# Dense batch 0 in units of 128 tokens, batches 1 to 3 of a block-sparse attention by lists of key blocks

## The chip, the core and the metric

The kernel runs on one core of one Trainium2 chip. The core has TensorE (PE, matmuls, with its weight loads shown apart as PEld), VectorE (DVE), ScalarE (ACT), GpSimd (POOL) and SyncE (SP, which here only issues DMAs). Each engine works through its own instructions in program order and waits on semaphores for the others. The metric is the device time of one execution in microseconds (us); less is better. Several executions of a kernel are timed, and the median is given with the lowest and the highest.

## What is computed

A BigBird-like attention over 4 batches, 8 heads, 768 tokens and head size 64, followed by a SwiGLU feed-forward network (FFN) on 3072 tokens of width 512.

```python
block, n_blocks, window = 32, 24, 1
scores = q @ k^T / sqrt(64)
mask = |blk_i - blk_j| <= 1
mask |= blk_i in (0, 23) or blk_j in (0, 23)
for qb in range(24):
    for kb in sampled_blocks[qb]:          # 3 per query block, drawn at random, an input
        mask[rows of qb, columns of kb] = True
attn = softmax(where(mask, scores, -1e9)) @ v
x = attn, heads side by side: [3072, 512]
xn = x / sqrt(mean(x*x) + 1e-6) * rms_g
out = (silu(xn @ w_gate) * (xn @ w_val)) @ w_out      # 512 -> 1536 -> 512
```

A query block of 1 to 22 thus sees at most 8 key blocks of 24: its own, two neighbours, blocks 0 and 23, and three sampled ones (which can coincide with the others). Blocks 0 and 23 see all keys. Inputs are fp32; matmuls are in bf16.

## The kernel before

**Tiling.** Tokens are laid out so that partition p of 128 holds the six tokens 6p to 6p+5 (`"b h (p c) d -> b p h (c d)"`, L66), and a tile c is one token of each partition. Work goes by units (L51): batch 0 has units of 1, 1, 1 and 3 tiles (128, 128, 128 and 384 tokens), batches 1 to 3 have two units of 384 tokens. A pair is two heads; there are four pairs.

**Attention is dense.** All 768 keys are scored for all queries, and the mask is put in by the matmul itself: to the 64 rows of K are appended 24 rows that say which block a key is in, and to those of Q 24 rows with 0 or -32768, so that the contraction has 88 rows (`KQ`). `qk` (L268) makes the scores in two PSUM banks, for 384 tokens one matmul of 384 columns per head and key tile; `exp` (L281) takes them through ACT into the tile `pt`, two heads x 384 columns at a time; `av` (L301) multiplies with V, which has a 65th column of ones that sums the probabilities; `xo` (L315) divides by that sum on DVE.

**Feeding it.** For batch 0, K and Q are cast into `aug` and transposed on TensorE (`tpx` L252, `evx` L261). For batches 1 to 3 they are loaded a pair at a time from SP's queue (`load` L76, 12 pairs x 3 loads), cast on DVE (`fill` L234, `pad_v` L238) and transposed by a DMA issued on SP (`turn` L244, 12 of them).

**FFN.** For each unit: `sq` (L326, DVE) and `rsq` (L339, POOL) make the norm, `xq` (L346, DVE) scales, the result is transposed on TensorE (`tr`, `cp`) for the first four units and by DMA (`xt` L373) for the rest. Then come steps f, each of 384 columns: `proj` (L380) with the gate weights into bank 4, `th` (L393, tanh on ACT), `uu` (L399, DVE, which frees bank 4), `proj` with the value weights into bank 5, `hp` (L407, DVE). `yy` (L418) and `yo` (L431) make and store the output. Near the end, when all scores are made, the banks of the scores serve the FFN too (L689).

**Order.** All of it is put in order by a planner in the kernel's Python (L458 to L768): each operation has a cost per engine, dependencies, a priority and buffers or banks that it takes and gives back; a list scheduler with assumed latencies (`LAT`, L455) picks the next operation, and the instructions are issued in that order. SP's queue has an order of its own (`seq`): loads of batch 0, then checks that weight chunks have landed (`gate_sync`, L218), then the loads of later batches, with output stores, transposes and these loads all behind one another. POOL issues the ten weight DMAs and casts a few tiles at the start; after that it only has `rsq`.

Of the kernel before, what the change touches and what calls it, by code (L numbers as in the profile page):

```python
# [17 lines left out]
def kernel(  # L18
# [11 lines left out]
):  # L30
    nc = tc.nc
    SIMOUT = None
# [12 lines left out]
    NSLOT, NAUG, NRAW, NOPEN = 5, 2, 3, 2  # L45
# [5 lines left out]
    UNITS = [(0, 0, 1), (0, 1, 1), (0, 2, 1), (0, 3, 3)]  # L51
    UNITS += [(b, c, 3) for b in range(1, B) for c in (0, 3)]
    NU = len(UNITS)
    HG = [(b, c // 3) for b, c, n in UNITS]
# [3 lines left out]
    raw = ctx.enter_context(tc.tile_pool(name="raw", bufs=NRAW))  # L58
    work = ctx.enter_context(tc.tile_pool(name="work", bufs=2))
    psum = ctx.enter_context(tc.tile_pool(name="psum", bufs=1, space=bass.MemoryType.PSUM))  # L60
    PS = psum.tile([P, 8, 512], FP32, name="PS")

# [7 lines left out]
    raws = {}  # L70
    aug = [const.tile([P, 2, 2, NC, P], BF16, name=f"aug{i}") for i in range(NAUG)]
    XA = const.tile([P, NSLOT, 2, 2, S], BF16, name="XA")
    X = [XA[:, i] for i in range(NSLOT)]
    vaug = [const.tile([P, H * NC, D + 2], BF16, name=f"vaug{i}") for i in range(2)]

    def load(g, i):  # L76
        b, pr = divmod(g, NP)
        if i == 0:
            raws[g] = raw.tile([P, 3, 2, NC * D], FP32, name="qkv", tag="qkv")
        nc.sync.dma_start(out=raws[g][:, i], in_=(kv, qv, vv)[i][b, :, 2 * pr:2 * pr + 2, :])  # L80
# [9 lines left out]
    A = [raw.tile([P, 3, 2, NC * D], FP32, name="qkv", tag="qkv") for g in range(3)]  # L90
# [23 lines left out]
    zt = const.tile([P, 512], BF16, name="zt")  # L114
# [11 lines left out]
    def idle(n, bk=7):  # L126
# [23 lines left out]
        base=-(NB - 1), pattern=[[0, 32]], channel_multiplier=1)  # L150
    kt_ = bank16(4)[:, 0:S].rearrange("p (c t) -> p c t", t=P)
# [8 lines left out]
    for t in vaug:  # L160
        nc.vector.memset(t[:, :, D:D + 1], 1.0)
# [72 lines left out]
    def fill(g, i, eng):  # L234
        copy(eng, aug[g % NAUG][:, i, :, :, 0:D],
             raws[g][:, i].rearrange("p h (c d) -> p h c d", d=D))

    def pad_v(g, eng):  # L238
        b, pr = divmod(g, NP)
        src = raws.pop(g) if b else A[g]  # L240
        copy(eng, vaug[b % 2][:, 2 * pr * NC:2 * (pr + 1) * NC, 0:D],
             src[:, 2].rearrange("p h (c d) -> p (h c) d", d=D))

    def turn(g):  # L244
        nc.sync.dma_start_transpose(
            out=X[g % NSLOT].rearrange("p i e (c t) -> p (i e c) t", t=P),
            in_=aug[g % NAUG].rearrange("p i e c r -> p (i e c r)"))

    def zero_pad(i):
        nc.vector.memset(aug[i][:, :, :, :, KQ:P], 0.0)  # L250
# [13 lines left out]

    pts, xos, xns, hps, mss, xqs, tiles = {}, {}, {}, {}, {}, {}, {}
    KT, FG = {1: 3, 2: 2, 3: 1}, {1: 3, 2: 2, 3: 1}

    def qk(u, pr, g, bk):  # L268
        b, c0, nt = UNITS[u]
        x, kt, w = X[(b * NP + pr) % NSLOT], KT[nt], nt * P  # L270
# [10 lines left out]
    def exp(u, pr, g):  # L281
        b, c0, nt = UNITS[u]
        kt, w = KT[nt], nt * P
        if (u, pr) not in pts:
            if nt == 1:
# [4 lines left out]
                else:  # L290
                    t_ = work.tile([P, 2, NC, 2, w], BF16, name="pt", tag="pt", bufs=NPT)
                pts[u, pr // 2 * 2], pts[u, pr // 2 * 2 + 1] = t_[:, 0], t_[:, 1]
            else:
                pts[u, pr] = work.tile([P, NC, 2, w], BF16, name="pt", tag="pt", bufs=NPT)
# [6 lines left out]
    def av(u, pr, bk):  # L301
        b, c0, nt = UNITS[u]
        pt, va = pts.pop((u, pr)), vaug[b % 2]
# [11 lines left out]
    def xo(u, pr):  # L315
        nt = UNITS[u][2]
        if u not in xos:
            xos[u] = work.tile([P, nt, H, D], FP32, name="xo", tag="xo")
# [7 lines left out]
    def sq(u, t):  # L326
# [5 lines left out]
        if nt == 1:  # L332
            z = (slice(0, 3 * DM // 4), slice(3 * DM // 4, DM))[t]
# [30 lines left out]
    def cp(u, eng):  # L364
# [3 lines left out]
        if eng == "ACT":  # L368
            nc.scalar.copy(out=o, in_=i)
        else:  # L370
            nc.vector.tensor_copy(out=o, in_=i)
# [428 lines left out]
```

## Time and profile before

| | |
|---|---|
| median of 3 runs | 309.45 us (308.69 to 309.54) |
| span of the profiled execution | 307.2 us |
| TensorE: granted clock | 0.999 |
| TensorE matmul busy, 30 to 60 us | 29.8 us |
| TensorE matmul busy, 130 to 210 us | 79.4 us |
| DMA engines busy in slices 2 to 16 of 40 (8 to 123 us) | 90% or more each |
| last matmul of the scores | 221.7 us |
| FFN alone after that | to 303.3 us |

The span is from the first to the last instruction of one execution; the timed median is a little longer than it. Busy times of an engine leave out instructions that only issue DMAs, except on POOL, where the issue is work of the engine. The group rows give, after the shapes and the count, the summed busy time, the mean duration of one in ns, and, after the second bar, the idle time of the engine just before them and what ended it.

### The profile page before, as it was taken

The numbers are of one execution on the slowest core, as the hardware profiler recorded it, in microseconds if no ns is written. First come the engines' busy times: TensorE is split into PE (matmuls) and PEld (weight loads), VectorE is DVE, ScalarE is ACT, GpSimd is POOL, SyncE is SP. The second block draws the span as 40 slices with busy tenths as digits, with TensorE's granted clock in tenths as the row PEclk, the third lists the DMA queues.
The fourth block names the chain that finished last, engine by engine and source line by source line (L and its number), as shares of the span: only waits on it lengthen the run. The fifth ranks groups of instructions, "written<-read, shape, count | busy, mean of one in ns | idle before, by whom it ended". The sixth has DMA issues, their size and how long they took to land.

```text
span 307.2 us, 7350 instructions
## 1 busy us (share of the span) xinstructions
PE 299.6 (98%) x3033; PEld 200.2 (65%) x3062; DVE 192.3 (63%) x435; ACT 203.7 (66%) x319; POOL 24.4 (8%) x43
## 2 busy tenths in 40 slices
PE   8999999999999999999999999999999999999994
PEld 7998888766666566666666666666666546556543
DVE  6687766857779678756754753674389607727500
ACT  5999875678977878787877787878833143233221
POOL 3566000100001001001000100010000000000000
PEclk9999999999999999999999999999999999999999
DMA  7999999999999999940894030003010050010022
GB/s 207 370 231 172 215 268 228 228 333 247 262 285 271 227 205 222 242 155 3 173 157 101 0 87 2 34 3 85 2 36 1 20 158 12 0 70 0 0 105 104
DMA packets 70661, 42.42 MB, mean 138 GB/s; under 512 B 48356, under 2 KB 67556, under 8 KB 70628
## 3 DMA queue, kind: packets, MB, share of 16 engines
q1 hardware_dynamic: 64528, 37.17, 49.2%
q0 software_dynamic: 5792, 4.72, 10.0%
q8 instruction: 24, 0.39, 0.6%
q10 hardware_dynamic: 308, 0.07, 0.1%
q14 instruction: 9, 0.07, 0.1%
HBM read 28.57 MB, written 6.29 MB: 114 GB/s over the span
## 4 chain that ended last, share of the span: by engine, by line
PE 96%; ACT 2%; issue 1%; DVE 0%; ACTq 0%
PE PS L388 40%; PE PS L276 20%; PE PS L427 20%; PE PS L310 12%; PE PS L258 2%; ACT pt L296 1%; PE PS L128 1%; PE PS L361 0%; ACT th L397 0%; PE PS L153 0%; ACT yo L437 0%; PE PS L183 0%; DVE zt L115 0%; ACTq L437 0%
## 5 line engine op out<-in xcount | busy, mean ns | idle before, releaser
L296 ACT ACTIVATE pt<-PS 128x768 bf16<-128x768 f32 x188 | 142.8, 812 | 32.2 <-PE PS L276 31.5
L403 DVE SCALAR_TENSOR_TENSOR uu<-th,PS 128x384 bf16<-128x384 bf16 x96 | 53.0, 554 | 58.7 <-ACT th L397 55.7
L276 PE MATMUL PS<-XA 88*128 88x384 bf16 (+1 forms) x480 | 81.1, 293 | 0.7 <-ACT pt L296 0.6
L388 PE MATMUL PS<-xn,wv 128*128 128x384 bf16 (+1 forms) x480 | 75.5, 293 | 0.0
L388 PE MATMUL PS<-xn,wg 128*128 128x384 bf16 (+1 forms) x480 | 75.1, 294 | 0.0
L397 ACT ACTIVATE th<-PS 128x384 bf16<-128x384 f32 x96 | 47.2, 493 | 34.8 <-PE PS L388 32.1
L427 PE MATMUL PS<-wo,hp 128*128 128x512 bf16 (+1 forms) x271 | 65.4, 370 | 1.5
L414 DVE TENSOR_TENSOR hp<-uu,PS 128x384 bf16<-128x384 bf16 x96 | 51.4, 551 | 14.2 <-PE PS L388 14.0
L388 PEld LDWEIGHTS <-wv 128*128 128x128 bf16 x480 | 41.6, 97 | 23.3
L388 PEld LDWEIGHTS <-wg 128*128 128x128 bf16 x480 | 41.4, 98 | 22.5
L276 PEld LDWEIGHTS <-XA 88*128 88x128 bf16 x480 | 39.2, 97 | 21.4 <-issue 1.8
L427 PEld LDWEIGHTS <-hp 128*128 128x128 bf16 x300 | 29.1, 98 | 27.0
L310 PEld LDWEIGHTS <-pt 128*128 128x128 bf16 x1128 | 40.5, 97 | 5.8
L310 PE MATMUL PS<-vaug,pt 128*128 128x65 bf16 x1128 | 42.1, 193 | 0.0
L437 ACT ACTIVATE yo<-PS 128x512 f32<-128x512 f32 (+1 forms) x22 | 12.7, 578 | 27.9 <-PE PS L427 27.2
L343 POOL TENSOR_TENSOR rs<-ms,nhalf 128x3 f32<-128x3 f32 (+1 forms) x10 | 7.9, 785 | 203.8 <-DVE ms L335 203.8
L322 DVE TENSOR_TENSOR xo<-PS,rz 128x384 f32<-128x384 f32 (+1 forms) x40 | 19.1, 478 | 1.4
L350 DVE SCALAR_TENSOR_TENSOR xq<-xo,rs,gB 128x512 bf16<-128x512 f32 x24 | 17.3, 747 | 2.3 <-POOL rs L343 2.3
L335 DVE CUSTOM_DVE_ANT_0 sc<-xo 128x512 bf16<-128x512 f32 (+1 forms) x24 | 16.1, 669 | 0.2
L321 DVE RECIPROCAL rz<-PS 128x6 f32<-128x6 f32 (+1 forms) x40 | 7.4, 186 | 12.8 <-PE PS L310 12.6
L112 DVE CAST aug<-qkv 128x768 bf16<-128x768 f32 (+1 forms) x28 | 14.5, 538 | 0.1
L112 DVE COPY XA<-PS 88x768 bf16<-88x768 bf16 (+2 forms) x17 | 8.4, 516 | 2.3 <-PE PS L258 2.2
(60 smaller groups left out, 74.5 us busy)
## 6 DMA issues: line engine op xcount, KB each, us to landing
out_dram<-yo SPq DMA_DIRECT2D x23, 256.0 KB, 2.4
qkv<-in_v_dram SPq DMA_DIRECT2D x15, 384.0 KB, 6.1
qkv<-in_k_dram SPq DMA_DIRECT2D x14, 384.0 KB, 5.6
qkv<-in_q_dram SPq DMA_DIRECT2D x12, 384.0 KB, 5.7
wg<-in_moe_w_gate_dram POOLq DMA_DIRECT2D x4, 384.0 KB, 7.3
wv<-in_moe_w_val_dram POOLq DMA_DIRECT2D x4, 384.0 KB, 8.4
wo<-in_moe_w_out_dram POOLq DMA_DIRECT2D x2, 768.0 KB, 19.0
q<-in_q_dram SPq DMA_DIRECT2D x1, 768.0 KB
```

The costliest lines, as they stand in the source:

```text
L112: nc.vector.tensor_copy(out=out, in_=in_)
L276: nc.tensor.matmul(out=s_[:, e, j * w:(j + 1) * w], lhsT=x[0:KQ, 0, e, jt * P:(jt + 1) * P], rhs=x[0:KQ, 1, e, c0 * P:c0 * P + w], start=T ...
L296: nc.scalar.activation(out=pts[u, pr][:, g * kt:(g + 1) * kt].rearrange("p j e w -> p e j w"), in_=s_[:, :, 0:kt * w].rearrange("p e (j w) ...
L310: nc.tensor.matmul(out=o_[:, t, e, :], lhsT=pt[:, jt, e, t * P:(t + 1) * P], rhs=va[:, (2 * pr + e) * NC + jt, 0:D + 1], start=(jt == 0), ...
L322: nc.vector.tensor_tensor(out=xos[u][:, :, 2 * pr:2 * pr + 2, :], in0=o_[:, :, :, 0:D], in1=rz.unsqueeze(3).to_broadcast([P, nt, 2, D]), o ...
L335: nc.vector.tensor_tensor_reduce(out=sc[:, z], in0=x, in1=x, scale=1.0 / DM, scalar=mss[u][:, 0:1] if nt == 1 and t else 1e-6, op0=ALU.mul ...
L350: nc.vector.scalar_tensor_tensor(out=xqs[u][:, t, :], in0=xos[u][:, t].rearrange("p h d -> p (h d)"), scalar=mss[u][:, t:t + 1], in1=gB, o ...
L388: nc.tensor.matmul(out=p_[:, j, :].rearrange("p (t w) -> p t w", w=P), lhsT=w_[:, c, f_ * P:(f_ + 1) * P], rhs=xns[u][:, :, c, :], start=( ...
L397: nc.scalar.activation(out=t_, in_=tiles["gp", u, f], func=AF.Tanh, scale=0.5)
L403: nc.vector.scalar_tensor_tensor(out=t_, in0=tiles.pop(("th", u, f)), scalar=1.0, in1=tiles.pop(("gp", u, f)), op0=ALU.add, op1=ALU.mult)
L414: nc.vector.tensor_tensor(out=hps[u][:, f * fg:(f + 1) * fg, :], in0=tiles.pop(("uu", u, f)), in1=tiles.pop(("vp", u, f)), op=ALU.mult)
L427: nc.tensor.matmul(out=tiles["yp", u, t, h], lhsT=hps[u][:, f, t * P:(t + 1) * P], rhs=wo[:, f, x], start=(f == 0), stop=(f == NF - 1))
```

## The change

Batch 0 keeps the dense code (renamed `dk`, `dexp`, `dav`, `dxo`) but has six units of 128 tokens in place of 128, 128, 128 and 384. Its three large probability tiles come from one fixed tile.

Batches 1 to 3 are sparse. Their tokens lie in natural order, 128 rows to a group; a group n is four query blocks: 4n+1 to 4n+4 for n from 0 to 4, and blocks 0, 23, 21, 22 for group 5 (`AT`). A batch has two units of three groups, (5, 0, 1) and (2, 3, 4).

- **Keys.** K of a batch is loaded whole (512-byte pieces), cast and transposed by one DMA (`turn_k`); two heads are stacked in the 128 rows. For each group a tile `kg` is filled by copies with six slots of 128 keys: slots 0 to 3 hold, for each query block, three sampled blocks and one neighbour; slots 4 and 5 hold, for each two query blocks, those two blocks and blocks 0 and 23. The sampled copies read K at an offset from a register, on POOL (samples 0 and 1) or ACT (sample 2).
- **Queries.** Q (256-byte pieces) is transposed on TensorE for batch 1 and by DMA for batches 2 and 3, and copied into a tile `QBD` with the two heads side by side and zeros in the other head's rows.
- **Scores and probabilities.** `qk` makes matmuls of 64 columns (slots 0 to 3) and 128 columns (slots 4 and 5). `exp` writes them into tiles that were set to zero once, so that queries a slot does not concern have probability zero. Group 5 scores all keys for blocks 0 and 23 (`qka`, `expa`).
- **Values.** V is cast, stored to DRAM as rows of 520 bf16 (8 heads of 64 and a one), and fetched back by list: a slot of 128 rows by one indirect DMA on POOL (`gather_v`), slots 4 and 5 by SP (`pair_v`). A sampled block that coincides with another of the list is pointed at a block of zero rows, which takes the place of the mask.
- **Table.** The row numbers (`idx`) are computed once on DVE and POOL, and 66 block offsets are loaded into registers of POOL (44) and ACT (22) near planned time 48 us.
- **Around it.** The square of `sq` may run on ACT; `rsq` has two instructions; `NXN` goes from 3 to 2; output of group 5 is stored in three pieces; six units (those of batch 0) transpose on TensorE.

```diff
-    UNITS = [(0, 0, 1), (0, 1, 1), (0, 2, 1), (0, 3, 3)]
-    UNITS += [(b, c, 3) for b in range(1, B) for c in (0, 3)]
+    DENSE = [(c, 1) for c in range(NC)]
+    UNITS = [(0, c, n) for c, n in DENSE]
+    for b in range(1, B):
+        UNITS += [(b, (5, 0, 1), 3), (b, (2, 3, 4), 3)]
...
+    def turn_k(b):
+        KTs[b] = KTB[held["KT", b][1]]
+        nc.sync.dma_start_transpose(
+            out=KTs[b].rearrange("p a (n x) -> p (a n) x", x=P), in_=KROW.rearrange("p a c t x -> p (a c t x)"))
...
+    def kg_sampled(b, n, xs, eng):
+        kg = new_kg(b, n).rearrange("p x a s j c -> p x a c s j")
+        kt = KTs[b].rearrange("p a (c y) -> p a c y", c=2)
+        for x, r in xs:
+            kb = koff[(blocks(n)[x] - 1) * NR + r]
+            copy(eng, kg[:, x, :, :, r, :], kt[:, :, :, bass.ds(kb, 16)])
...
+    def gather_v(b, n, x):
+        c_ = blocks(n)[x] - 1
+        nc.gpsimd.indirect_dma_start(
+            out=new_vg(b, n)[:, x, :], out_offset=None, in_=vrows[b][:, :],
+            in_offset=bass.IndirectOffsetOnAxis(ap=idx[:, c_:c_ + 1], axis=0))
...
+    def qk(b, n, pp, bk):
+        s_ = PS[:, bk[0]:bk[0] + 2].rearrange("p k (h x) -> p (k h) x", h=2)
+        tiles["s", b, n, pp] = s_
+        kg = kgs[b, n].rearrange("p x a s j c -> p x a (s j c)")
+        qb = tiles["qb", b, n]
+        for pl in range(2):
+            pr = 2 * pp + pl
+            o_ = s_[:, 2 * pl:2 * pl + 2]
+            for i in range(4):
+                qmm(o_[:, :, i * 32:(i + 1) * 32], kg[:, i, pr], qb, i, 1, pr)
+            for g in range(2):
+                lo = P + g * 64
+                qmm(o_[:, :, lo:lo + 64], kg[:, 4 + g, pr], qb, 2 * g, 2, pr)
...
+    def av(b, n, pp, bk):
+        p_, vg = pts.pop((b, n, pp)), vgs[b, n]
...
+        for a in range(4):
+            h = 4 * pp + a
+            if n == AT:
+                vs = [vaug[:, m % 3, m // 3, h, :] for m in range(NC)]
+                vs += [vg[:, x, h * (D + 1):(h + 1) * (D + 1)] for x in (2, 3, 5)]
+            else:
+                vs = [vg[:, x, h * (D + 1):(h + 1) * (D + 1)] for x in range(6)]
+            for x, v_ in enumerate(vs):
+                nc.tensor.matmul(
+                    out=o_[:, a, :], lhsT=p_[:, a, x * P:(x + 1) * P], rhs=v_,
+                    start=(x == 0), stop=(x == len(vs) - 1))
...
-        nc.gpsimd.tensor_tensor(out=r, in0=x, in1=nhalf[:, 0:nt], op=ALU.pow)
+        nc.gpsimd.tensor_scalar(out=r, in0=x, scalar1=1e-6, scalar2=None, op0=ALU.add)
+        nc.gpsimd.tensor_tensor(out=r, in0=r, in1=nhalf[:, 0:nt], op=ALU.pow)
...
+    done0 = [("av", u, pr) for u in (ND - 2, ND - 1) for pr in range(NP)]
...
+    for i in range(NPT + 1 + NQB):
+        op(("zr", i), {"DVE": 1.3, "POOL": 1.9} if i <= NPT else {"DVE": 0.7, "POOL": 1.1},
+           done0 if i <= NPT else [("dk", ND - 1, 2, ng3 - 1)], (3.5, i), lambda e, p, i=i: zero(i, e))
...
+            op(("pvi",) + T, {"SP": 2.0}, [("st", b)], (1.1, order),
+               lambda e, p, a=T: pair_v(*a), [("vg", T)])
...
+            for x in xs:
+                op(("gv",) + T + (x,), {"POOL": 1.05}, [("st", b), ("ix", 7)], (1.1, order, x),
+                   lambda e, p, a=T + (x,): gather_v(*a), [("vg", T)])
+                op(("gd",) + T + (x,), {"DMA": 0.4}, [("gv",) + T + (x,)], (-1, order, x), None)
```

## The prediction

> **What bounds the kernel now.** I read the page's busy shares first, then the chain that ended last, then the groups with shapes kept apart, then the chain in order of time for the price of single matmuls.
>
> ```profile
> span 307.2 us, 7350 instructions
> PE 299.6 (98%) x3033; PEld 200.2 (65%) x3062; DVE 192.3 (63%) x435; ACT 203.7 (66%) x319; POOL 24.4 (8%) x43
> ...
> PE PS L388 40%; PE PS L276 20%; PE PS L427 20%; PE PS L310 12%; PE PS L258 2%; ACT pt L296 1%; PE PS L128 1%; PE PS L361 0%; ACT th L397 0%; PE PS L153 0%; ACT yo L437 0%; PE PS L183 0%; DVE zt L115 0%; ACTq L437 0%
> ```
>
> TensorE works 98% of the span and is 96% of the chain. 7.6 us are left to idling. So a microsecond of matmul removed is a microsecond won, as long as the next engine in line keeps TensorE fed.
>
> ```profile
> 31.70 1.15 PE PS L310 x36
> 32.85 0.65 PE PS L276 x4
> ...
> 27.61 0.67 PE PS L388 x12
> ...
> 241.07 10.31 PE PS L427 x47
> ```
>
> In the chain by time (start, duration, what) I take prices of single matmuls: 65 columns with a new weight each 1.15/36 = 0.032 us; 384 columns 0.65/4 = 0.1625; 128 columns 0.67/12 = 0.056; 512 columns 10.31/47 = 0.219. The means in the groups (325 ns for 384 columns) are latencies of overlapping matmuls and would double the sum.
>
> ```profile
> L296 ACT ACTIVATE pt<-PS 128x768 bf16<-128x768 f32 x188 | 142.8, 812 | 32.2 <-PE PS L276 31.5
> L403 DVE SCALAR_TENSOR_TENSOR uu<-th,PS 128x384 bf16<-128x384 bf16 x96 | 53.0, 554 | 58.7 <-ACT th L397 55.7
> L397 ACT ACTIVATE th<-PS 128x384 bf16<-128x384 f32 x96 | 47.2, 493 | 34.8 <-PE PS L388 32.1 <-ACT pt L296 0.2
> L322 DVE TENSOR_TENSOR xo<-PS,rz 128x384 f32<-128x384 f32 x28 | 15.6, 557 | 1.0
> L343 POOL TENSOR_TENSOR rs<-ms,nhalf 128x3 f32<-128x3 f32 x7 | 6.1, 878 | 199.7 <-DVE ms L335 199.7
> L211 POOL DMA_DIRECT2D wg<-in_moe_w_gate_dram x4 | 3.3, 818 | 0.0
> L110 POOL CAST aug<-qkv 128x256 bf16<-128x256 f32 x1 | 0.4, 400 | 0.4 <-DMA qkv<-in_q_dram 0.4
> ```
>
> These rows price the other engines. POOL is all but idle now (8%); the change hands it the most.
>
> **TensorE, batches 1 to 3.** Removed: 3 batches x 2 units x 4 pairs x 2 heads x 6 key tiles = 288 score matmuls of 384 columns, 288 x 0.1625 = 46.8 us. Added per batch: five ordinary groups with, per pair, 4 matmuls of 64 columns and 2 of 128, so 4 x (4 x 0.032 + 2 x 0.056) = 0.96 us each, 4.8 in all; the group with blocks 0 and 23 has per pair 7 of 128 and 2 of 64, 4 x 0.456 = 1.8. That is 6.6 a batch, 19.9 for three. **Saving 26.9.** AV grows from 288 to 5 x 48 + 72 = 312 matmuls a batch: 72 x 0.032 = +2.3. Q of batch 1 is now transposed on TensorE: 24 x 0.056 = +1.3. K of 128 rows (was 88) costs nothing: the AV rows have 128 and are the price used.
>
> **TensorE, batch 0.** Unit 3 (384 tokens) becomes three of 128: 96 projections 15.6 -> 288 x 0.056 = 16.1, and 48 scores 7.8 -> 144 x 0.056 = 8.1: +0.8. Sum: 299.6 - 26.9 + 2.3 + 1.3 + 0.8 = 277.1 us. With the 7.6 of idle as now the span is 284.7. The shown median, 309.45, is 2.25 above this execution's span; I carry that over: **286.9 if nothing else idles TensorE**. The FFN and the tail of outputs are unchanged.
>
> **What must keep pace with it.** TensorE has per sparse batch 192 x 0.1625 + 72 x 0.219 + 6.6 + 312 x 0.032 = 63.5 us (71.9 now). Against that:
> ACT. Two rows (384 columns 493 ns, 768 columns 812) give 0.174 + 0.83 ns per column, so 512 columns 0.60, 256 0.39, 128 0.28. Exps: 20 x 0.60 + 4 x (0.60 + 0.39 + 0.28 + 0.28) = 18.2 a batch (48 x 0.76 = 36.5 now). Added: third sampled key, 11 operations of two 128-column copies, 22 x 0.28 = 6.2. With tanh 24 x 0.49 and outputs 6 x 0.6: 39.8.
> DVE. uu and hp 24 x 1.105 = 26.5; xo, now 12 of 256 columns, 12 x (0.19 + 0.42) = 7.4, with 0.42 between the 128-column (291 ns) and 384-column rows; squares and scaling 6 x (0.77 + 0.75) = 9.1: 43.0.
> POOL. Sampled keys 22 operations of two copies, 44 x 0.30 = 13.2 (from 400 ns for 256 columns and 507 for 384); rsq, now two instructions, 2 x (0.88 + 0.4) = 2.6; 22 gathers. No row shows an **indirect DMA**: the least is a plain weight DMA issued on POOL (0.74), the most, far away, the issue of a transposing DMA on SP (median 4.37, where the issuer makes all its pieces). A gather is one DMA with one index per partition, nearest to the plain one; I take 1.05, 23.1 a batch: 38.9.
> Free to go to any of the three: casts of K, V, Q, fixed key copies, diagonal Q, about 7 + 7.7 + 4.9 = 19.6 us. In all 141 of 3 x 63.5 = 191 engine-us, 74%. Now ACT is at 52 of 71.9 and DVE at 48. So no engine binds by its total. They serve as cover as long as the gathers stay below 2.2 us, where 15.8 + 22 x 2.2 passes 63.5.
>
> ```profile
> 46.05 10.53 SPq L245 DMA_TRANSPOSE XA<-aug  x2
> ...
> 57.99 0.39 SPq L80 DMA_DIRECT2D qkv<-in_k_dram  x1
> ```
>
> **The SP queue** gains. A transposing DMA holds it for 3.6 to 6.2 us, and 12 of them become 5: 7 x 4.4 = 31 us less. Against that come, per batch, 10 loads (12 now), one store of V, 12 pair and end-block copies and 2 more output pieces: 13 more of 0.45, 6 us. The pair copies wait in that queue for a V buffer and for the store; queued behind them are next-batch loads and outputs, whose landing is needed a block later. At zero, as SP has gaps of 14 us and more after 130 us.
> **Register loads.** 66 block offsets, 22 on ACT and 44 on POOL, near 48 us. No row shows one; least 0.10 (POOL's smallest memset), most 0.44 (an SP issue): 2.2 to 9.7 us on ACT. I take 5, hidden since ACT is busy 5.4 of 10 from 50 to 60; without that cover it delays the exps of batch 0 by 5. The table itself, some 30 small DVE operations at 0.16, is 5 us in a stretch where DVE has 2 to 3 of 10 free.
>
> **The hand-over to batch 1** is the new wait I charge. The first sparse scores wait for the last dense AV (the zeros in the shared probability tiles, about 3 us on two engines), then 11 us of exps for three groups, 3 for AV and xo, 5 for square, power and scaling, 4 for the transpose: 26 us before unit 6 has an FFN. Cover: FFN of units 4 and 5, 2 x 8 = 16 us of TensorE, and 9 us of its own sparse attention. But with one bank for g, a step lasts 0.67 + 0.2 + 0.49 + 0.16 + 0.55 + 0.08 = 2.15 us for 1.34 of matmul (0.2, 0.16 and 0.08 are the planner's latencies), so the cover is leaky: 4 us, bounds 0 (unit 7's attention fills it) and 16 (K, V and Q of batch 1 land late). Uneven fit over 18 groups: 2 us, bounds 0 and 9 (half a DVE instruction per group; the static order was exact to 0.5% until now). 286.9 + 4 + 2 = **293**.
>
> [...] POOL's weight DMAs took 0.74 to 0.95 us beside a DVE at 7.6 of 10. [...]
>
> **Rivals.**
> 1. The chain g-th-uu in its one bank sets the pace. A step of 384 tokens is 0.65 + 0.2 + 0.49 + 0.16 + 0.55 + 0.08 = 2.13 us, 25.6 for the 12 of a unit, and TensorE has 31.8. With one and a half foreign DVE instructions of 0.55 ahead of each uu it is 2.95 x 12 = 35.4: 3.6 x 4 interleaved units = 14 us on 288: 302. For: DVE gets more, smaller work. Against: before, 3 us a step was kept with TensorE above 99%.
> 2. POOL binds (slower). Gathers can start near 50 us; three batches take 3 x (15.8 + 22 g); after the last come about 33 us of attention and FFN. 130 + 66 g passes 309.45 at g = 2.7; at the row's upper end of 4.37 it is 418, and I price the rival a little past its threshold, at 3: 328. For: 66 operations with no row behind them. Against: the plain issues at 0.8.
> 3. Batch 1 is late. Its loads now run in pieces of 256 and 512 bytes (1536 now), each group needs all of K, Q and stored V, and DMA is above 90% busy from 8 to 123 us: 16 us of idle instead of 4, 305.
> 4. Small matmuls don't shrink: at 0.1 each the 468 new scores cost 46.8, and the time is 314. The 0.032 rows speak against it; I fold it into the second.
>
> **Chances.** Forecast 0.50 (own range 284 to 300), rival 1 0.15, rival 2 with 4 0.23, rival 3 0.12. Changes under 0.3% can't be told from none. Faster: 0.49 + 0.11 + 0.01 + 0.09 = 0.70; same 0.03; slower 0.27. The range goes from 283, every bound in favour, less 4 for better packing, to 314, which takes in rivals 1 and 3 and the low edge of 2.
>
> **What would show it.** Scores of batches 1 to 3 near 20 us on TensorE, its busy time near 277; exps near 55 us there; gathers near 1.05 on POOL; an idle hole of TensorE between 60 and 85 us no longer than 6. Wrong: gathers over 2.2, TensorE below 93%, or waits for POOL key copies in the chain.

## The result: 349.43 us, and the profile after

The changed kernel takes 349.43 us (median of 4 runs, 346.68 to 352.56), the kernel before beside it 309.07: a ratio of 1.128 (95% interval 1.122 to 1.134). The ratios in this text leave out executions more than 1.5% above their kernel's fastest, the medians do not. The forecast was 293, its range 283 to 314. The profiled execution has a span of 346.2 us. First the page of the kernel after: span, busy shares, the chain that ended last, three groups.

```profile
span 346.2 us, 9294 instructions
...
PE 295.3 (85%) x3625; PEld 211.6 (61%) x3625; DVE 208.2 (60%) x525; ACT 187.0 (54%) x417; POOL 155.7 (45%) x294
...
PE 59%; DVE 9%; issue 5%; another core or an unknown queue 3%; ACT 2%; DMA 1%; ACTq 0%; DVEq 0%
...
L741 DVE SCALAR_TENSOR_TENSOR uu<-th,PS 128x384 bf16<-128x384 bf16 x96 | 52.8, 552 | 44.6 <-ACT th L735 38.3
L547 POOL DMA_INDIRECT VGC<-vrows,idx x66 | 64.5, 977 | 27.9 <-issue 13.8
...
L752 DVE TENSOR_TENSOR hp<-uu,PS 128x384 bf16<-128x384 bf16 x96 | 51.3, 551 | 29.7 <-remote 13.1
```

TensorE is busy 4.3 us less than before (295.3 against 299.6), not 22.5, and idle 50.9 us (346.2 - 295.3) where it was idle 7.6. `uu` takes 552 ns (554 before). No other engine took TensorE's place: POOL, the fullest by the change, is at 45%; its power for three tiles (`rs`) takes 940 ns (878 before). The gathers cost POOL what was said (0.977 us each). New in the page is "remote": VectorE stood 13.1 us before `hp` for an event of which the profile knows no source.

The groups of the kernel after with shapes kept apart:

```profile
L607 ACT ACTIVATE PTC<-PS 128x512 bf16<-128x512 f32 x60 | 33.2, 599 | 16.4 <-remote 6.4 <-PE PS L580 3.5 <-PE PS L726 3.5
L659 DVE TENSOR_TENSOR XO<-PS,rz 128x256 f32<-128x256 f32 x36 | 15.3, 425 | 1.2
L634 ACT ACTIVATE PTC<-PS 128x512 bf16<-128x512 f32 x12 | 7.2, 602 | 8.7 <-PE PS L580 6.4 <-remote 2.3
L684 POOL TENSOR_TENSOR rs<-rs,nhalf 128x3 f32<-128x3 f32 x6 | 5.6, 940 | 0.5
L634 ACT ACTIVATE PTC<-PS 128x128 bf16<-128x128 f32 x24 | 5.3, 275 | 1.0 <-PE PS L580 0.7 <-issue 0.4
L634 ACT ACTIVATE PTC<-PS 128x256 bf16<-128x256 f32 x12 | 4.7, 388 | 0.3 <-PE PS L580 0.3
```

The unit costs were right: 512 columns of exp take 599 ns (0.60 forecast), 256 take 388 (0.39), 128 take 275 (0.28), 256 columns of `XO` on DVE 425 (0.42), and the exps of batches 1 to 3 sum to 33.2 + 7.2 + 5.3 + 4.7 = 50.4 us (54.6 forecast). Start to start, a score matmul of 64 columns takes 29 ns and one of 128 takes 56: 264 and 204 of them make 19.1 us (19.9 forecast). So no unit was dear in itself; the time went into waits. They are of two kinds.

**A hole at the hand-over.** The timeline of the kernel after from 50 to 59 us (start, duration, what; in brackets the idle time before it and what ended it):

```profile
44.00 15.18 SPq L471 DMA_TRANSPOSE XC<-AUG  x1
...
53.32 1.61 POOL L142 CAST vaug<-RAWC 128x768 bf16<-128x768 f32 x2 [9.35 <-DMA RAWC<-in_v_dram]
...
56.22 0.57 POOL L684 TENSOR_TENSOR rs<-rs,nhalf 128x1 f32<-128x1 f32 x1
...
56.82 0.75 DVE L691 SCALAR_TENSOR_TENSOR xq<-XO,rs,gB 128x512 bf16<-128x512 f32 x1 [7.33 <-POOL rs L684]
...
58.49 0.80 PE L726 MATMUL PS<-xn,wg 128*128 128x128 bf16 x6 [7.53 <-DVE uu L741]
```

GpSimd stands 9.35 us before the cast of batch 1's V, which is still on its way. Behind that cast in GpSimd's queue is the power for batch 0's norm (`rs`), VectorE waits for it with `xq`, and `uu` is behind `xq`: TensorE idles 7.53 us.

**Completions that come late.** The timeline of the kernel after from 80 to 88 us:

```profile
80.97 0.83 PE L726 MATMUL PS<-xn,wg 128*128 128x128 bf16 x12
81.44 0.98 POOL L547 DMA_INDIRECT VGC<-vrows,idx  x1 [0.30 <-issue]
81.64 0.83 PE L726 MATMUL PS<-xn,wv 128*128 128x128 bf16 x12
82.31 0.81 PE L765 MATMUL PS<-wo,hp 128*128 128x512 bf16 x3
82.72 0.95 POOL L547 DMA_INDIRECT VGC<-vrows,idx  x1 [0.30 <-issue]
82.74 0.49 ACT L735 ACTIVATE th<-PS 128x384 bf16<-128x384 f32 x1 [1.09 <-PE PS L726]
...
83.98 0.95 POOL L547 DMA_INDIRECT VGC<-vrows,idx  x1 [0.30 <-issue]
85.02 0.56 DVE L752 TENSOR_TENSOR hp<-uu,PS 128x384 bf16<-128x384 bf16 x1 [4.30 <-remote]
...
85.62 0.83 PE L726 MATMUL PS<-xn,wv 128*128 128x128 bf16 x12 [2.50 <-issue]
```

The value matmuls are recorded from 81.64 to 82.48 us. `hp`, whose other input has been ready since 80.71, starts at 85.02. The semaphore by which TensorE reports its work counted up at 84.92, 2.44 us after the end on record, and with the end of the gather that began at 83.98. Over the run 70 of TensorE's some 440 reports that can be matched with a recorded end came over 0.3 us late, in 22 clusters whose longest delays sum to 40.7 us; all 22 lie beside runs of gathers. In the kernel before none is late. Of the other engines' reports none that can be matched is late in either kernel, but beside the gathers some have no record at all (37 of ACT's 335, 30 of VectorE's 446, 10 of GpSimd's 160, and 17 of TensorE's 462), and none is missing in the kernel before.

TensorE itself pauses too: 18 times, 10.0 us in sum, it stands over 0.15 us before a matmul that waits for no semaphore on record, each time beside gathers; the kernel before has one such pause, of 0.2 us. So the hold is more than a late report. All this is a coincidence in one trace; the experiments had to make it a cause.

In five holes, or within 1.3 us of their end, TensorE's granted clock fell to 0.50 for a while (23.9 us in sum: 10.24 us from 53.2 us, and 3.41 us each from 90.8, 148.8, 159.0 and 179.5 us; none before; the very end of each trace apart). Four gate matmuls of 384 columns take 1.47 us there (from 150.08 us), and 0.81 at a granted 1.00 (from 163.19 us).

### The profile page after: what moved, and what is told of

Its sections match the earlier page's. It is cut to its first block, busy times and chain, and to the rows that moved or that the text cites. A ratio compares the mean times of both kernels' runs of the same rounds, so it can differ in the third digit from the quotient of the medians.

```text
span 346.2 us, 9294 instructions
## 1 busy us (share of the span) xinstructions
PE 295.3 (85%) x3625; PEld 211.6 (61%) x3625; DVE 208.2 (60%) x525; ACT 187.0 (54%) x417; POOL 155.7 (45%) x294
## 4 chain that ended last, share of the span: by engine, by line
PE 59%; DVE 9%; issue 5%; another core or an unknown queue 3%; ACT 2%; DMA 1%; ACTq 0%; DVEq 0%
PE PS L726 28%; PE PS L765 16%; PE PS L649 9%; PE PS L580 4%; DVE hp L752 2%; PE PS L578 2%; DMA xn<-xq 1%; DVE XO L659 1%; DVE uu L741 1%; ACT PTC L634 1%; DVE AUG L144 1%; DVE KGC L144 1%; DVE XC L144 1%; DVE rz L658 1%
## 5 line engine op out<-in xcount | busy, mean ns | idle before, releaser
L726 PE MATMUL PS<-xn,wg 128*128 128x128 bf16 (+1 forms) x576 | 78.8, 281 | 12.6 <-DVE uu L741 8.9
L726 PE MATMUL PS<-xn,wv 128*128 128x128 bf16 (+1 forms) x576 | 77.9, 278 | 7.6 <-DVE hp L752 4.1
L547 POOL DMA_INDIRECT VGC<-vrows,idx x66 | 64.5, 977 | 27.9 <-issue 13.8
L752 DVE TENSOR_TENSOR hp<-uu,PS 128x384 bf16<-128x384 bf16 x96 | 51.3, 551 | 29.7 <-remote 13.1
L726 PEld LDWEIGHTS <-wg 128*128 128x128 bf16 x576 | 46.6, 101 | 33.8 <-issue 16.9
L142 POOL COPY KGC<-XC 128x128 bf16 (+1 forms) x147 | 46.4, 385 | 12.4 <-PE PS L578 5.6
L649 PEld LDWEIGHTS <-PTC 128*128 128x128 bf16 x936 | 35.1, 100 | 19.8 <-issue 15.7
L607 ACT ACTIVATE PTC<-PS 128x512 bf16<-128x512 f32 x60 | 33.2, 599 | 16.4 <-remote 6.4
L649 PE MATMUL PS<-VGC,PTC 128*128 128x65 bf16 x792 | 35.1, 196 | 7.8 <-DVE XO L659 3.9
L318 ACT ACTIVATE PTC<-PS 128x768 bf16<-128x768 f32 x44 | 33.3, 821 | 2.5 <-PE PS L297 2.4
L140 ACT COPY KGC<-XC 128x128 bf16 (+2 forms) x95 | 29.8, 401 | 8.1 <-PE PS L726 3.3
L297 PE MATMUL PS<-XC 88*128 88x128 bf16 x288 | 22.2, 218 | 0.7 <-ACT PTC L318 0.7
```

The costliest lines, as they stand in the source:

```text
L140: nc.scalar.copy(out=out, in_=in_)
L142: nc.gpsimd.tensor_copy(out=out, in_=in_)
L318: nc.scalar.activation(out=pts[u, pr][:, g * kt:(g + 1) * kt].rearrange("p j e w -> p e j w"), in_=s_[:, :, 0:kt * w].rearrange("p e (j w) ...
L547: nc.gpsimd.indirect_dma_start(out=new_vg(b, n)[:, x, :], out_offset=None, in_=vrows[b][:, :], in_offset=bass.IndirectOffsetOnAxis(ap=idx[ ...
L607: nc.scalar.activation(out=o_, in_=i_, func=AF.Exp, scale=SCALE)
L649: nc.tensor.matmul(out=o_[:, a, :], lhsT=p_[:, a, x * P:(x + 1) * P], rhs=v_, start=(x == 0), stop=(x == len(vs) - 1))
```

## The experiments

Theory G: the indirect gathers hold TensorE back, and this is most of the loss. Theory L: the late load of V with work queued behind it is the rest. Against G stand S (any DMA issued on GpSimd does it) and P (GpSimd and VectorE are too busy or in the wrong order). In all kernels below the transposing DMAs are plain copies of the same bytes between the same tiles; those built on the kernel before have the mask set to nothing as well. The runs came in five sets, each on one chip with the kernel before beside it: set 1 on chip A, 2 on B, 3 on C, 4 on D, 5 on A again.

### Set 1: base, copies for gathers, the late load, gathers in the kernel before

```diff
-        nc.sync.dma_start_transpose(
-            out=KTs[b].rearrange("p a (n x) -> p (a n) x", x=P), in_=KROW.rearrange("p a c t x -> p (a c t x)"))
+        nc.sync.dma_start(
+            out=KTs[b].rearrange("p a (n x) -> p (a n x)", x=P), in_=KROW.rearrange("p a c t x -> p (a c t x)"))
...
```

> The kernel after, with its 11 transposing DMAs (K and Q of a batch, x of a unit) replaced by plain copies of the same bytes between the same tiles on the same queue; what is multiplied is therefore not the transposed data. It is the base for the runs beside it. If the transposing DMAs have no part in the loss (theories G and L): 342 to 353 us, TensorE's late completions beside the runs of gathers near 40 us in sum, the hole at 51 us there. Rival T (a transposing DMA and a gather by index get in each other's way): 300 to 315 us, no late completions.

Measured: 350.09 us (347.92 to 352.26), 65 late reports, clusters of 42.3 us. A part of the transposing DMAs in the loss doesn't show.

```diff
-            in_offset=bass.IndirectOffsetOnAxis(ap=idx[:, c_:c_ + 1], axis=0))
+        lo = 32 * min(blocks(n)[x], NB - 4)
+        nc.gpsimd.dma_start(out=new_vg(b, n)[:, x, :], in_=vrows[b][lo:lo + P, :])
```

> The run with copies in place of the transposing DMAs, and each of the 66 indirect gathers replaced by a plain copy of 128 consecutive rows (same bytes, same tile, issued by GpSimd too, same place in the order) with a block start fixed in the program; V of the listed blocks is therefore not the right one either. Theory G (the gathers by index on GpSimd hold TensorE's completions back, some 0.5 to 0.6 us for each): 308 to 318 us, and no completion of TensorE more than 0.3 us late. Rival S (any transfer that GpSimd starts does it): 340 to 350 us, late completions as before. Rival P (GpSimd and VectorE are too busy or in the wrong order, whatever kind the transfers are): within 5 us of the base.

Measured: 307.32 us, ratio to the kernel before 0.992 (0.987 to 0.997), no late report at all. The same bytes, packets, tiles, queue and order, issued by the same engine: 42.8 us are gone. S falls. P is not quite out by this run, since a copy takes GpSimd 564 ns where a gather takes 981, and its busy time goes from 155.6 to 127.2 us; the runs on the kernel before, below, settle it. The stretches of the two kernels (from:to, length, TensorE busy and its instructions, granted clock, DMA share, GB/s) show where; with gathers (the base):

```profile
80.00:120.00 40.00, 28.22 (x499) 1.00 0.64 167
120.00:160.00 40.00, 31.87 (x408) 1.00 0.88 238
160.00:240.00 80.00, 64.75 (x821) 0.91 0.50 145
```

and with copies:

```profile
80.00:120.00 40.00, 35.70 (x607) 1.00 0.93 253
120.00:160.00 40.00, 37.00 (x528) 0.96 0.92 258
160.00:240.00 80.00, 78.75 (x958) 1.00 0.43 130
```

It is made where the gathers run, 80 to 250 us. The base's TensorE is idle 350.6 - 292.3 = 58.3 us, that of the copies 309.8 - 283.8 = 26.0; the busy times differ by 8.5, and the base has 20.5 us at half clock against 13.7. The execution with copies that was profiled took 311.55 us, one of the longer ones of its kernel, so the difference is rather too small here.

```diff
-                lat = LLAT
+                lat = {"k": 7.0, "v": 14.0}.get(k_[1], LLAT) if k_[2] == 1 else LLAT
```

> The run with copies in place of the transposing DMAs, and the planner told that V of batch 1 lands 14 us after its issue and its keys 7 us after, where it assumed 6 for both; nothing else changes. Theory L (the hole of 7.5 us at 51 us, and the half clock after it, come from GpSimd's cast of V that waits for a late load with the work of the queries queued behind it): 6 to 11 us under the base, the hole gone, the sum of late completions still near 40 us. Rival: the time is made up later or moves to another wait: within 3 us of the base.

Measured: 353.84 us (352.52 to 355.16), 87 late reports. Not faster. The hole moved from 51 to 58 us, as the timeline of this run shows:

```profile
61.69 0.87 ACT L140 COPY KGC<-XC 128x256 bf16<-128x256 bf16 x3 [5.35 <-issue]
...
64.05 1.22 PE L726 MATMUL PS<-xn,wg 128*128 128x128 bf16 x10 [6.16 <-DVE uu L741]
```

Now the key copies, which need the turned K, stand at the head of ACT's and DVE's queues, with `th` and `uu` behind them. L as a cure falls: late data has more than one queue to stand in.

```diff
+    for i in range(NG):
+        op(("sg", i), {"POOL": 1.25}, [("sr",)], (6, i), lambda e, p, i=i: spare_gather(i),
+           at=90.0 + 8.0 * (i // 4) + 1.25 * (i % 4))
...
```

> The kernel before, with its 18 transposing DMAs replaced by plain copies of the same bytes and the mask set to nothing (the copied data is not transposed and no block is masked), and 66 indirect gathers added on GpSimd, of the same size and pattern of index as the kernel after has, in runs of four from about 90 us on, into a buffer that nothing reads. Theory G: 335 to 350 us, TensorE's completions late beside the runs of gathers. Rivals by which GpSimd's or VectorE's load, or the order of the sparse batches, made the loss: within 3 us of 309.

Measured: 321.72 us (320.66 to 322.78), 29 late reports, clusters of 11.4 us. The kernel before, with no sparse work in it, gets late reports from gathers that nothing reads. The copies and the missing mask are not it: a run of set 5 with the same two edits, batch 0 in six units and no gathers takes 309.77 us. But 12 us is far from 335 to 350, and 5.3 of it is a single hole where a `rs` on GpSimd stood behind gathers that waited for their two buffers. These waits also broke up the runs: 24 gathers followed another directly (within 0.4 us), 48 in the kernel after.

### Set 2: planned landings, SyncE's copies, long runs, runs broken up

```diff
-                lat = LLAT
+                b_ = k_[2] if k_[0] == "l" else k_[1]
+                lat = {"k": 11.0, "v": 18.0, "lq": 8.0}[k_[1] if k_[0] == "l" else "lq"] if b_ == 1 else LLAT
...
```

> As the run with all 66 gathers replaced by plain copies on GpSimd (307.3 us), and the planner told longer landings for what batch 1 needs: 11 us for its keys, 18 for V, 8 for Q and for the turn of K, where it assumed 6, 6, 6 and 4; its own plan then ends at 302.8 us instead of 299.0. What is multiplied is again neither the transposed data nor the listed V. Theory L2 (with the gathers gone, what is left over the plan is in-order engines standing before batch 1's late loads, with work of batch 0 queued behind, and the half clock after it): 300 to 304 us, no hole of TensorE over 2 us between 40 and 75 us, clock near 1.0. Rival (the loads are late by the DMA's own limit, and moving the waits only moves the loss): 306 to 311 us.

Measured: 315.17 us, ratio 1.025 (1.017 to 1.032). A miss, and slower than its base of 307.3 (on chip A, 0.992 of the kernel before there). Its stretches:

```profile
40.00:60.00 20.00, 18.11 (x347) 1.00 1.20 247
60.00:80.00 20.00, 11.62 (x153) 0.83 0.43 98
```

The hole between 40 and 60 us is filled (18.11 us busy; 12.65 in the base with copies, 13.93 in the run with SyncE's copies below, which is on this chip), and 60 to 80 loses 3.4 against the one and 6.8 against the other (15.00 and 18.43): what is planned later is missing later.

```diff
-        nc.gpsimd.dma_start(out=new_vg(b, n)[:, x, :], in_=vrows[b][lo:lo + P, :])
+        nc.sync.dma_start(out=new_vg(b, n)[:, x, :], in_=vrows[b][lo:lo + P, :])
```

> As the run with plain copies on GpSimd (307.3 us), but the 66 copies are issued by SyncE. If that run's remaining loss were GpSimd's work, this one is faster by several us: 300 to 304. Otherwise 305 to 311 us. No late completions either way; should rows of 1,040 bytes written from another queue hold TensorE, over 330.

Measured: 307.08 us (306.05 to 308.68), no late report. GpSimd does 32 us less and nothing is won: its load is not what remains. That no report is late says little here, since on this chip gathers held none either (next two runs).

```diff
-    VW, NG = H * (D + 1), 66
-    gbuf = const.tile([P, 2, VW], BF16, name="gbuf")
+    VW, NG = H * (D + 1) // 2, 66
+    gbuf = const.tile([P, 4, VW], BF16, name="gbuf")
```

> The kernel before with copies for its transposing DMAs, no mask, and 66 added gathers as in the run of 321.7 us, with two changes: rows of 520 bytes instead of 1,040, and four buffers instead of two, so that no gather waits for the landing of the one two before it and the runs of four stand back to back (there 24 of the 66 did, in the kernel after 48). If what is held grows with the length of a run: 330 to 350 us, holds above 2 us. If it goes by the bytes moved: 313 to 318 us. If by the number of gathers alone: 320 to 323 us.

Measured: 308.29 us (307.9 to 309.07), no late report, though 55 of the 66 gathers followed another directly.

```diff
+                op(("gs",) + T + (x,), {"GAP": 0.9}, [("gv",) + T + (x,)], (-1, order, x), None)
+                glast = T + (x,)
...
```

> The kernel after with copies for its transposing DMAs (350.1 us), and a planned pause of 0.9 us of GpSimd's time after each gather, so that other work of GpSimd comes between most of them (20 gathers follow another directly, 48 before). If runs of gathers hold TensorE's completions longer than single ones do: 322 to 338 us, holds mostly under 2 us. If each gather costs the same wherever it stands: 346 to 353 us. If the pause only delays V: over 353.

Measured: 318.99 and 326.17 us, no late report. I first read the two together: short rows don't hold, and neither do short runs. But this set was on another chip than the first, and neither run had a control on it. The two times of the second are too far apart to stand for one number.

### Set 3: the control

> The run of 350.1 us again (the kernel after, copies for its transposing DMAs, so that what is multiplied is not the transposed data), beside the two below, because the last four runs were on another chip than the first four. If runs of gathers are what holds TensorE's completions, on any chip: 342 to 354 us, with late completions. If the hold belongs to the chip of the first four runs: 315 to 326 us, no late completions, as the spread one had.

> The run of 322.6 us again (copies for the transposing DMAs; a planned pause of 0.9 us after each gather), on the chip of its neighbours. If the runs' length is the cause: 317 to 328 us and no late completions on any chip. If it is the chip: 340 to 355 us where the one beside it is at 342 to 354.

> The run of 321.7 us again (the kernel before with copies for its transposing DMAs, no mask, and 66 added gathers of rows of 1,040 bytes in runs of one to three). If the hold is a matter of chance or of the chip: 307 to 310 us with no late completions where the first one beside it has none either. If it is the kernel: 319 to 324 us.

Measured on chip C: the base 345.9 us (64 late reports, clusters of 40.4 us), the one with runs broken up 334.35 (334.21 to 334.48; 41 late, 19.9), gathers in the kernel before 319.41 (34 late, 12.0). So breaking up the runs takes 11.5 us off on one chip, less than was expected (317 to 328 us), and the absence of any hold in set 2 was not the kernels' doing. One run of eight gathers stayed together there, from 235 to 245 us, and beside it stands the longest hold of all:

```profile
239.07 1.12 PE L726 MATMUL PS<-xn,wg 128*128 128x384 bf16 x4
...
246.98 0.49 ACT L735 ACTIVATE th<-PS 128x384 bf16<-128x384 f32 x1 [6.13 <-remote]
```

The gate matmuls end at 240.19 us on record, TensorE's count goes up at 246.90, 6.7 us later, and `th` starts; beside that kernel's other gathers, alone or up to three together, no report is more than about 2 us late.

### Set 4: control and long runs side by side, lists by SyncE, light loads

> The run of 350.1 us once more (the kernel after, copies for its transposing DMAs, not the transposed data), as the control of the chip it shares with the three below. On a chip that holds TensorE's completions: 343 to 353 us with late completions. On a chip that does not, as the third to eighth runs' neighbours had it: 308 to 322 us with none, which would put the whole of the stall on the chip and its gathers together.

> The run of 308.3 us again (the kernel before with copies for its transposing DMAs, no mask, and 66 added gathers of rows of 520 bytes, back to back in long runs), since that run's chip may not hold completions at all. Where the control beside it shows late completions: by length of run 325 to 350 us; by bytes 307 to 318 us with few late completions. Where the control shows none, this run says nothing.

Measured on chip D: the control 350.98 us (64 late, 46.6), and long runs in the kernel before **369.64** (369.28 to 370.0), the kernel that took 308.29 on chip B. That is above the 325 to 350 expected. Short rows are no protection, the loss goes with the length of the runs, and on chip B nothing was held. GpSimd has the same work on both chips, so its load, the last of P, is not it. Here too TensorE pauses without a wait (15 times, 13 of them beside gathers, 10.4 us; never on chip B). In the middle of one AV group, beside four gathers from 187.38 to 192.08 us:

```profile
187.82 0.49 PE L327 MATMUL PS<-vaug,pt 128*128 128x65 bf16 x9
188.83 0.21 PE L327 MATMUL PS<-vaug,pt 128*128 128x65 bf16 x1 [0.52 <-issue]
189.55 0.23 PE L327 MATMUL PS<-vaug,pt 128*128 128x65 bf16 x1 [0.50 <-issue]
190.24 0.22 PE L327 MATMUL PS<-vaug,pt 128*128 128x65 bf16 x1 [0.46 <-issue]
191.63 0.27 PE L327 MATMUL PS<-vaug,pt 128*128 128x65 bf16 x2 [1.17 <-issue]
```

Where 36 of these matmuls took 1.15 us in the kernel before, in these lines one or two start every 0.7 to 1.4 us, and they wait for no semaphore on record.

```diff
+        _, got_ = nc.values_load_multi_w_load_instructions(
+            vti[0:1, c_ * NR:c_ * NR + NR], engines=[nc.sync.engine], min_val=0, max_val=32 * NB,
+            skip_runtime_bounds_check_because=WHY)
+        for r in range(NR):
+            nc.sync.dma_start(out=vg[32 * r:32 * r + 32, x, :], in_=vrows[b][bass.ds(got_[r], 32), :])
...
```

> The kernel after with copies for its transposing DMAs, and each gather by index replaced by four copies of 32 rows issued by SyncE, three with a row number that SyncE loads into a register from the table; the V that is multiplied is the listed one, K and Q are not transposed. Theory G (only the gathers by index on GpSimd hold TensorE): 304 to 312 us, no late completions. Rival (264 small copies and 198 register loads in SyncE's one queue come late, and V with them): 318 to 335 us, TensorE waiting for V.

Measured: 420.76 us (418.21 to 422.87), no late report, on a chip where the control has 64: V by list without gathers holds nothing, as G says. But the time is the rival's, and worse than it said. What TensorE waits for in this run (total, times, longest):

```profile
PE PS L656 <- DMA VGC<-vrows: 80.3, 33, 4.9
```

The planner took these copies for work of GpSimd and put nothing for them on SyncE, where they stand in one queue with loads that wait for their buffers. An order that plans them there wasn't run, so whether V by list can be had cheaply without gathers is open.

```diff
-            in_=kvv[i][b, :, 3 * HH * hf:3 * HH * (hf + 1), :])
+            in_=kvv[i][b, :, 3 * HH * hf:3 * HH * hf + (1 if b == 1 else 3 * HH), :])
...
```

> The run with plain copies on GpSimd in place of the gathers (307.3 us), with only a twelfth of batch 1's K and V and an eighth of its Q loaded (the rest of these tiles is zero, cleared by GpSimd between 14 and 30 us; neither transposed data nor the listed V nor the whole of batch 1's inputs is used). Theory L3 (the idle of TensorE between 40 and 80 us, 12 us there, and the half clock after it are batch 1's loads landing late among other transfers): 294 to 301 us, TensorE idle under 4 us between 40 and 80 us. Rival (the order of the conversions makes the hole, whenever the loads land): 304 to 309 us.

Measured: 305.23 us, ratio 0.989 (0.982 to 0.996), which can't be told from the 0.992 of its base on chip A; again no late report, on a chip that holds. Its stretches:

```profile
40.00:60.00 20.00, 18.19 (x347) 1.00 0.97 204
60.00:80.00 20.00, 15.40 (x198) 0.91 0.56 148
```

With a twelfth of K and V to load, the hole before 60 us is gone (18.19 us busy for 12.65), but 60 to 80 us is about as idle as in the base's profiled execution (15.40 against 15.00). TensorE is idle 6.4 us between 40 and 80 us, not under 4, mostly waiting for `uu` (4.6 us), which stands on VectorE behind casts and the table's operations. The chain there goes over two register loads of GpSimd (3.67 us from 64.95 and 2.71 from 68.70) and key copies to the first sparse scores at 75.8 us. So the rival fits, the order of the conversions: late loads made one hole, and with that gone the hand-over shows another. Whether every kernel with copies has both isn't shown; the run with SyncE's copies is busy 18.43 us from 60 to 80.

### Set 5: single gathers, and batch 0 alone

> The run of 308.3 and then 369.6 us once more, as the control of the chip that the run with single gathers is on (the kernel before with copies for its transposing DMAs, no mask, 66 added gathers of rows of 520 bytes in long runs). A chip that holds completions: 360 to 375 us; one that does not: 307 to 310.

```diff
-    gbuf = const.tile([P, 4, VW], BF16, name="gbuf")
+    gbuf = const.tile([P, 1, VW], BF16, name="gbuf")
...
```

> As the run beside it (the kernel before with copies for its transposing DMAs, no mask, 66 added gathers of rows of 520 bytes), but all gathers write one buffer, so that each waits for the landing of the one before it and none follows another directly. On a chip that holds completions: if it is the runs that hold, 307 to 315 us with hardly a completion over 1 us late; if every gather costs the same (60 us by 66 there), over 350 us; if a gather alone costs what one of a pair did (0.19 us), 319 to 323 us.

Measured on chip A: long runs 370.05 us (36 late, 33.4 us), single gathers 325.21 (324.61 to 325.81; 6 late, 2.6 us, none by more than 0.81). The time did not come down as far as the runs theory said, but what is left is no hold. (The planner also spaces these gathers 3.3 us apart, from 70 us on.) The waits of the run with single gathers:

```profile
DVE xq L367 <- POOL rs L360: 17.2, 5, 8.7
```

GpSimd waits for the landings (153.3 us for 63 of them, the longest 5.8), and the norm's `rs` stands behind: a cost of my edit (the chain has 27% in those landings). By its late reports a gather alone holds next to nothing.

The same instructions on two chips, at about 101 us. On chip B (first run of long runs):

```profile
101.37 0.82 PE L293 MATMUL PS<-XA 88*128 88x384 bf16 x4
...
101.90 3.17 ACT L313 ACTIVATE pt<-PS 128x768 bf16<-128x768 f32 x4 [0.44 <-PE PS L293]
```

and on chip A (third run of them):

```profile
100.59 0.81 PE L293 MATMUL PS<-XA 88*128 88x384 bf16 x4
...
104.55 0.95 POOL L244 DMA_INDIRECT gbuf<-spare,gidx  x1 [0.30 <-issue]
105.81 0.95 POOL L244 DMA_INDIRECT gbuf<-spare,gidx  x1 [0.30 <-issue]
106.79 0.20 DVE L338 RECIPROCAL rz<-PS 128x6 f32<-128x6 f32 x1 [5.88 <-remote]
106.83 1.51 ACT L313 ACTIVATE pt<-PS 128x768 bf16<-128x768 f32 x2 [7.00 <-remote]
...
107.69 1.50 PE L293 MATMUL PS<-XA 88*128 88x384 bf16 x4 [4.99 <-issue]
```

On B the exp starts 0.53 us after its first score matmul. On A it starts 6.24 us after. TensorE idles 4.99 and goes on at 107.69, 0.05 us after the first of these exps is done, which frees its bank.

```diff
-    UNITS = [(0, 0, 1), (0, 1, 1), (0, 2, 1), (0, 3, 3)]
+    UNITS = [(0, c, 1) for c in range(6)]
```

> The kernel before with copies for its transposing DMAs and no mask (nothing is transposed or masked), and batch 0 in six units of 128 tokens as the kernel after has them; batches 1 to 3 stay dense. By the prediction's step for batch 0 (more, smaller matmuls: 0.8 us): 308.5 to 311 us. If small units starve TensorE by more hand-overs: over 314 us.

Measured: 309.77 us (309.5 to 310.51), ratio 1.0005 (0.997 to 1.004). Batch 0's new units cost nothing that can be told from none; the 0.8 us of the forecast is inside. The plain copies and the missing mask, which this run shares with the runs of the kernel before that have gathers, cost nothing that shows either.

The runs made to vary the gathers, together ("directly": gathers that follow another within 0.4 us; "late": reports over 0.3 us late; "held": sum of the longest delay of each cluster). Where reports have no record the match is partly a choice: another way of matching moves the late ones by up to 10 and the sums by up to 4 us.

| run | chip | time, us | directly | late | held, us |
|---|---|---|---|---|---|
| after, base with copies | A | 350.1 | 48 | 65 | 42.3 |
| the same | C | 345.9 | 48 | 64 | 40.4 |
| the same | D | 351.0 | 48 | 64 | 46.6 |
| after, runs broken up | C | 334.4 | 20 | 41 | 19.9 |
| the same | B | 319.0 and 326.2 | 20 | 0 | 0 |
| before, long runs | D | 369.6 | 58 | 40 | 30.4 |
| the same | A | 370.1 | 57 | 36 | 33.4 |
| the same | B | 308.3 | 55 | 0 | 0 |
| before, two buffers, short runs | A | 321.7 | 24 | 29 | 11.4 |
| the same | C | 319.4 | 28 | 34 | 12.0 |
| before, single | A | 325.2 | 0 | 6 | 2.6 |

## Why the prediction was wrong

**The step that failed: "They serve as cover as long as the gathers stay below 2.2 us".** The gathers were charged to GpSimd alone. At 0.977 us they were even cheaper than the 1.05 taken, and by that step harmless. They cost TensorE 42.8 us of the 56 missed (350.1 to 307.3 us when plain copies stand in their place), by late reports, pauses and the half clock after them, and they do it in the kernel before as well, where nothing reads what they fetch (309.4 to 370.1 us). The sum had no term for a cost of gathers on an engine that doesn't run them. The second rival had the right instruction and sign, and the wrong mechanism: it asked for a gather above 2.7 us and a full GpSimd, which is at 45%.

**The hand-over, 4 us, and the uneven fit, 2 us.** With copies in place of gathers 307 us remain, 14 above the forecast. In the run with SyncE's copies TensorE is idle 304.4 - 283.0 = 21.4 us where the sum has 7.6 + 4 + 2 = 13.6: 7.6 us between 40 and 80 us (one hole of 6.0 at 51), 6.2 from 80 to 160. So in this one trace the hand-over was put at about half of what it is and the fit at a third. The bounds (16 and 9) held. The third rival named the late, finely cut loads; they do make the first hole, yet taking them away won 2 us by the medians, which can't be told from nothing, and that its 305 is near the time of the copies is partly luck.

**TensorE's busy time, 277.1.** In that run it is 283.0. Its 6.8 us at half clock explain an estimated 6.8 x (1 - 0.81/1.50) = 3.1 of the 5.9, if all matmuls stretch there as four score matmuls do (1.50 us for 0.81 in the last fence of set 5, at half clock). I charged no clock to holes; the rest stays open.

**What was right.** Scores 19.1 us for 19.9, exps 50.4 for 54.6, gathers 0.977 for 1.05, batch 0's units. Of the signs given for an error, TensorE below 93% came (85%), gathers above 2.2 and waits for key copies in the chain did not. The small matmuls did shrink, against the fourth rival. ACT's register loads took 4.95 us (5 taken); GpSimd's, which had no price of their own, took 11.1, starting from 56.2 to 69.5 us. The gathers took these 0.977 us beside a VectorE busy 60% of the span.

**SyncE's queue, at zero.** The turn of batch 1's K held it 15.18 us from 44.00, where 3.6 to 6.2 were counted; with a plain copy in its place the time stayed at 350.1 us, so nothing shows against the zero.

**Open.** What in an indirect gather holds TensorE, and why it doesn't on chip B. Whether length of run or the number of gathers under way at once counts: one, two and four buffers differ in both. Whether the products are in PSUM when the recorded end says so, since the profile models the ends of matmuls. And every timed execution here was also profiled, so what the gathers cost without recording isn't shown. The base built on the kernel after wasn't run on B, and which chip timed the kernel after isn't on record. No run computes the reference faster than the kernel before: the 305 to 307 us belong to kernels that fetch V at fixed places and transpose nothing by DMA.

## What to carry to other kernels

Price a new kind of instruction not only on the engine that runs it: look at whether others keep their pace and report on time beside it, by an engine waiting for "remote", by a matmul whose consumer starts long after its recorded end, and by gaps marked "issue" inside a group. Replacing indirect gathers by plain copies of the same bytes is a quick way to see what they cost. Where they hold TensorE, other GpSimd work between them helped here (11.5 us on chip C); making each wait for the one before all but ended the hold (2.6 us for 33.4 on chip A) and cost time elsewhere (17.2 us of VectorE behind `rs`). And a result from one chip, a hold or its absence, needs a control on the same chip (long runs took 308.3 us on B, 369.6 on D). A cast that stood in GpSimd's queue before its data was there delayed the unrelated work behind it (9.35 us of GpSimd, 7.53 of TensorE); planning it later moved the hole from 51 to 58 us (353.84 us for 350.09), so look first at what work beside it can fill it.

## What the hardware showed that I had not expected

Beside runs of gathers TensorE's reports came up to 6.7 us after the recorded end, and TensorE paused up to 1.46 us (kernel after) before matmuls that wait for no semaphore on record. Some matmuls beside gathers keep their pace (four in 0.82 and 0.81 us in the two fences of set 5). What makes the pauses isn't shown.

One kernel took 308.3 us on one chip and 369.6 and 370.1 on two others, while the kernel before stayed within 309.1 to 309.4 on all three.

Half clock came on top of the holes: in the third run of long runs TensorE is 368.6 - 323.4 = 45.2 us idle, 39.8 more than on chip B (306.6 - 301.2), and 22.2 us longer busy, with 58 us at half clock (mean granted clock 0.920, and 1.000 on B).
